# Splitting the first matmul of block 0 into three single-pass products, and re-timing the weight conversion's buffers, in a fused attention + FFN + FFN kernel

## The chip, the cores and the metric

One core of a Trainium2 chip (trn2) runs the whole program. The metric is device time in microseconds; the kernel before has a median of 902.7 us over three runs (900.95 to 904.78).

## What is computed

Pooled attention gives x (2304 tokens by 512), which goes through two feed-forward layers. Cut to what matters:

```python
k_p = k.reshape(B, H, Sp, 8, D).mean(axis=3); v_p = ...
attn = softmax(scale * q @ k_p^T);  x = attn @ v_p          # 2304 x 512
h = x @ moe_w_in;   g = where(h >= 1, h, where(h <= -1, 0, (h + 1)**2 / 4));  x = g @ moe_w_out
h = x @ moe2_w_in;  g = max(h, 0) + log1p(exp(-|h|));                         out = g @ moe2_w_out
```

Weights are 512 x 2048 and 2048 x 512. They arrive as 64-bit words, so each value has to be put together on ScalarE, VectorE (and GpSimd for the second layer) before TensorE can use it.

## The kernel before

The tokens are cut into five blocks (`BLK`: 4, 4, 4, 3, 3 tiles of 128 tokens). For each block, the first layer walks over 16 chunks of 128 hidden units. Chunk c of block j is iteration n = 16j + c of the main loop (L773). One iteration issues, on TensorE, the products of h (`emit_g1`, L496: four tiles of 128 along d_model) and then, two chunks late, the products of y (`emit_g2`, L537). Between them stand the activation (`act`, L516) and whatever `background` (L749) has due in that half step: two half steps `hs` make an iteration.

Block 0 is different (`whole`, L492). Its products use the fp32 weights and fp32 x as they are, one fp32 matmul per 128 x 128 weight tile, which the profile shows as two records each. From block 1 on each product is made of three matmuls of rounded parts (type fp32r): weight high by x high, weight high by x low, weight low by x high. The parts of a weight come from `split1` (L154): a copy with rounding on ScalarE (`whi`, L158), then a subtraction on VectorE (`wlo`, L160). In the kernel before, `split1` runs once per iteration: for the first two weight halves at the end of block 0, for the other 14 in block 1.

During block 0 the first layer's weights are also converted (`convert1`, L140): two ScalarE operations (L113, L116), then five on VectorE (L120, L121, L125, L148, L150) for each half weight. Each half weight is loaded by `w_load`; even and odd halves in `USE` (L133) belong to w_in and w_out in turn. Half `m` odd (m = 2i - 1) is needed by the products of h of chunks 2i and 2i + 1. The attention of block 1 (`tile_gen`, L400) and the pooling of the next batch's keys and values (`kv_gen`, L377; the reductions are L345) run between these operations.

From half step `CONV2` = 54 on, the second layer's weights are converted in 32 units (`convert2`, L174). `tick` (L667) advances the units under a budget of VectorE/ScalarE time (`credit`), starting a new one every `PITCH` = 3.1 half steps, if fewer than four of its buffers are in `held`. Each unit takes a buffer `a` (four of them); two units of w_in also make four sums in a tile `t` (L203 to L207). Every result is split into a high part in `b` (three buffers, L237) and a low part written over its source (L228), and both are stored to HBM (`wid`, `wod`) from the SP queue (L232 for the high part, L222 for the low part one tick later), because the second layer (L841 on) reads them from there (`wi_load`, `wo_load`). `held` drops a buffer as soon as its store has been issued. The tiles `t`, and all weights, take slots of one pool of 33 (`slot`).

All engines run in the order in which this program is written (`manual_schedule`), so an instruction that waits holds all that stands behind it on its engine. The pool's slots and the buffers make an instruction wait until the last reader of the earlier contents, stores included, is done.

Of the kernel before, what the change touches and what calls it, by code (L numbers as in the profile page):

```python
# [7 lines left out]
FP32 = mybir.dt.float32  # L8
FP32R = mybir.dt.float32r
# [3 lines left out]
ACTF = mybir.ActivationFunctionType  # L13
# [17 lines left out]
def pooled_attention_ffn_ffn(ctx, tc, q, k, v, v0, w1, w2, out):  # L31
# [24 lines left out]
    )  # L56

    CONV2, PITCH = 54, 3.1

    BUDGET = ((0.0, 0.0), (1.0, 2.5), (1.2, 2.5), (0.9, 1.9), (0.9, 1.9))  # L60
    T0 = [sum(BLK[:j]) for j in range(NB)]
# [41 lines left out]
    wi = {}  # L103
    wo = {}
    x2 = {}

    def slot(shape, dtype, name):
        return wpool.tile(shape, dtype, tag="w", name=name)
# [45 lines left out]
    def split1(m):  # L154

        hi, lo = (slot([128, 2, DM], FP32R, n) for n in ("whi", "wlo"))
        f = wt[USE[m]]
        nc.scalar.activation(out=hi, in_=f, func=ACTF.Copy)  # L158
        yield
        nc.vector.tensor_tensor(out=lo, in0=f, in1=hi.bitcast(FP32), op=ALU.subtract)  # L160
        wt[USE[m]] = (hi, lo)
        yield
# [6 lines left out]
            nc.sync.dma_start(out=raw[n], in_=src)  # L169

    left = {}
    held = []

    def convert2(n):  # L174
# [12 lines left out]
        st_load(n + 2)  # L187
        yield 0.7
        af = a.bitcast(FP32)
        nc.vector.tensor_tensor(out=af, in0=af, in1=l, op=ALU.add)  # L190
        yield 0.8 if r and not part else 0.0
        if part:
            jobs = [(n, af, lambda m: [(wod[:, h, m, r, :], slice(0, DM))])]
        elif r == 0:
            left[h] = af
            return
        else:

            b0, b1 = left.pop(h), af
            b11, b21, b12, b22 = (b[:, o:o + QK] for b in (b0, b1) for o in (0, QK))  # L200
            t = slot([128, 4, QK], FP32, "t")
            t3, t2, t4, t1 = (t[:, m, :] for m in range(4))
            nc.vector.tensor_tensor(out=t1, in0=b12, in1=b11, op=ALU.subtract)  # L203
            nc.vector.tensor_tensor(out=t3, in0=b22, in1=b12, op=ALU.subtract)
            yield 0.8
# [3 lines left out]
            tf = t.rearrange("p m f -> p (m f)")  # L209
            jobs = [  # L210
                (n - 1, b0, lambda m: [(wid[:, h, o, m, :], slice(x, x + QK)) for o, x in ((0, 0), (5, QK))]),
                (None, tf[:, 0:2 * QK], lambda m: [
                    (wid[:, h, 1 + o, m, :], slice(o * QK, (o + 1) * QK)) for o in range(2)]),
                (None, tf[:, 2 * QK:4 * QK], lambda m: [
                    (wid[:, h, 3 + o, m, :], slice(o * QK, (o + 1) * QK)) for o in range(2)]),
                (n, b22, lambda m: [(wid[:, h, 6, m, :], slice(0, QK))]),
            ]
        old = done = None
        stores = []
        for k, f, dst in jobs + [(None, None, None)] * 2:  # L220
            for d, x in stores:
                nc.sync.dma_start(out=d, in_=x)  # L222
            if done is not None:
                held.remove(done)
            stores, done = [], None
            if old:
                done, fo, hi, to = old
# [3 lines left out]
                for d, x in to(0):  # L231
                    nc.sync.dma_start(out=d, in_=hi.bitcast(FP32)[:, x])  # L232
                stores = [(d, fo[:, x]) for d, x in to(1)]
                old = None
            if f is not None:
                hi = es2.cv.tile([128, DM], FP32R, tag="b", bufs=3, name="b")[:, 0:f.shape[1]]
# [255 lines left out]
    def whole(j):  # L492

        return j == 0

    def emit_g1(j, c):  # L496
        n = 128 * BLK[j]
        h = ps["h"].tile([128, TB], FP32, tag="h", name="h")[:, 0:n]
        done = 0
        for kk in range(KD):  # L500
            cols = slice(kk * 128, (kk + 1) * 128)
            if whole(j):
                ops = ((wt[0, c // 2][:, c % 2, cols], xs[j][0].bitcast(FP32)),)
            else:
                wh, wl = (t[:, c % 2, cols] for t in wt[0, c // 2])
                xh, xl = xs[j]
                ops = ((wh, xh), (wh, xl), (wl, xh))
            for a, b in ops:
                nc.tensor.matmul(  # L509
                    out=h, lhsT=a, rhs=b[:, kk, 0:n],  # L510
                    start=(done == 0), stop=(done == len(ops) * KD - 1),
                )
                done += 1
        return h
# [150 lines left out]
    credit = [0.0]  # L665

    def tick(start):  # L667
        late = False
        for item in list(flight):
            late = late or item[1] > credit[0]  # L670
            if not (late and item[1]):
                credit[0] -= item[1]
                item[1] = next(item[0], None)
                item[2] += 1
                if item[1] is None:
                    flight.remove(item)
# [86 lines left out]

    pend = []
    acts = {}
    splits = []

    def step(key):
# [4 lines left out]
    for n in range(NB * NC):  # L773
# [20 lines left out]
            step(n - 2)  # L794
        if hot and c + 1 < NC:
            next(c1[c + 1])
        if hs == CONV2 - 4:
            st_load(0)
            st_load(1)
# [116 lines left out]
```

## Time and profile before

| | |
|---|---|
| median of 3 runs | 902.7 us (900.95 to 904.78) |
| the profiled execution | 907.54 us |
| its span (first to last instruction) | 905.7 us |
| TensorE busy | 878.4 us, 97% |
| TensorE weight load | 717.3 us, 79% |
| VectorE busy | 636.3 us, 70% |
| ScalarE busy | 508.4 us, 56% |
| GpSimd busy | 44.9 us, 5% |
| mean granted TensorE clock | 0.988 |

TensorE is busy for nearly all of the span, so the time can fall in two ways only: fewer microseconds of matmuls, or fewer of the gaps in which TensorE waits. A gap's row in the timeline names the instruction that ended it. A busy TensorE may also run at half its clock (the column PEclk).

### The profile page before, as it was taken

The page shows a single profiled execution, that of the slowest core. Times are in us where ns is not written, and L with a number is a line of the kernel's source. Part 1 is how long each engine was busy: PE and PEld are TensorE (multiplying, and loading weights), DVE is VectorE, ACT ScalarE, POOL GpSimd, SP SyncE. Part 2 cuts the span into 40 slices and gives each one's busy share as a digit, 9 for nine tenths or more (in the row PEclk, how much of TensorE's full clock was granted, in tenths as well). Part 3 has the DMA queues.
Part 4 walks back from the last instruction along what each step waited for, and adds up shares of the span by engine and source line. Part 5 has one row for each costly group of instructions (what it writes and reads, how often), then busy time and mean ns, then how long its engine had stood idle before and what let it go on. Part 6 is the DMA issues. An engine that isn't in the chain of part 4 may idle for free. (4 is left out here: it accounts for less than half of the span.)

```text
span 905.7 us, 12186 instructions
## 1 busy us (share of the span) xinstructions
PE 878.4 (97%) x4490; PEld 717.3 (79%) x4490; DVE 636.3 (70%) x951; ACT 508.4 (56%) x925; POOL 44.9 (5%) x41
## 2 busy tenths in 40 slices
PE   8899999999998999999999999999999999999996
PEld 4444445688886788889999988889899898889885
DVE  6798774665667768677888678585778766665763
ACT  3856653555654546656577565554657464554551
POOL 0000000000111112111121100000000000000000
PEclk8999999999999999999999999999999999999999
DMA  7745330110164545743585796548197456496202
GB/s 255 286 156 190 124 141 10 60 59 12 59 187 136 177 140 166 227 160 99 199 307 193 253 338 234 175 137 312 51 346 258 128 163 233 151 357 203 92 1 70
DMA packets 66411, 154.94 MB, mean 171 GB/s; under 512 B 6896, under 2 KB 27376, under 8 KB 64304
## 3 DMA queue, kind: packets, MB, share of 16 engines
q1 hardware_dynamic: 66352, 154.17, 50.4%
q8 instruction: 35, 0.57, 0.3%
q14 instruction: 24, 0.20, 0.1%
HBM read 121.63 MB, written 32.51 MB: 170 GB/s over the span
## 5 line engine op out<-in xcount | busy, mean ns | idle before, releaser
L590 PE MATMUL h<-xfh,wi 128*128 128x384 f32 x544 | 160.3, 337 | 1.9 <-DVE h L858 1.2
L627 PE MATMUL y<-whi,gl 128*128 128x512 f32 x288 | 114.1, 396 | 0.0
L627 PE MATMUL y<-wlo,gh 128*128 128x512 f32 x288 | 113.7, 395 | 0.0
L627 PE MATMUL y<-whi,gh 128*128 128x512 f32 x288 | 112.0, 389 | 0.0
L590 PEld LDWEIGHTS h<-xfh,wi 128*128 128x128 f32 x544 | 100.8, 188 | 9.4 <-DVE h L858 2.6
L551 PE MATMUL y<-gl,whi 128*128 128x512 f32 (+1 forms) x256 | 95.1, 371 | 9.7 <-DVE gl L535 9.6
L551 PE MATMUL y<-gh,whi 128*128 128x512 f32 (+1 forms) x256 | 96.0, 375 | 0.5 <-ACT gh L533 0.5
L509 PE MATMUL h<-xh,whi 128*128 128x512 f32 (+1 forms) x256 | 95.4, 372 | 0.0
L551 PE MATMUL y<-gh,wlo 128*128 128x512 f32 (+1 forms) x256 | 93.9, 367 | 0.0
L509 PE MATMUL h<-xh,wlo 128*128 128x512 f32 (+1 forms) x256 | 92.8, 362 | 0.0
L509 PE MATMUL h<-xl,whi 128*128 128x512 f32 (+1 forms) x256 | 92.7, 362 | 0.0
L590 PE MATMUL h<-xfl,wi 128*128 128x384 f32 x272 | 91.9, 338 | 0.0
L601 ACT ACTIVATE e<-h 128x768 f32<-128x768 f32 x48 | 40.1, 840 | 84.2 <-DVE h L858 84.2
L858 DVE TENSOR_TENSOR h<-h,s 128x384 f32<-128x384 f32 x72 | 40.0, 556 | 65.8 <-PE h L590 65.6
L519 ACT ACTIVATE t<-h 128x512 f32<-128x512 f32 (+1 forms) x80 | 44.0, 550 | 61.5 <-PE h L509 60.0
L185 POOL TENSOR_TENSOR l<-l,st 128x512 bf16<-128x512 bf16 x32 | 43.5, 1360 | 465.0 <-DVE st L125 410.7
L627 PEld LDWEIGHTS y<-whi,gl 128*128 128x128 f32 x288 | 54.0, 187 | 11.6
L551 PEld LDWEIGHTS y<-gl,whi 128*128 128x128 f32 x256 | 48.8, 191 | 17.3 <-DVE gl L535 12.7
L509 PE MATMUL h<-xh,wf 128*128 128x512 f32 x128 | 59.4, 611 | 0.7 <-ACT xh L479 0.7
L627 PEld LDWEIGHTS y<-whi,gh 128*128 128x128 f32 x288 | 54.1, 188 | 6.3
L627 PEld LDWEIGHTS y<-wlo,gh 128*128 128x128 f32 x288 | 54.0, 187 | 6.3
L551 PE MATMUL y<-g,wf 128*128 128x512 f32 x128 | 58.1, 596 | 0.4 <-DVE wf L150 0.4
(96 smaller groups left out, 1666.2 us busy)
## 6 DMA issues: line engine op xcount, KB each, us to landing
wi<-wid SPq DMA_DIRECT2D x72, 512.0 KB, 5.4
raw<-in_w SPq DMA_DIRECT2D x16, 1024.0 KB, 4.8
st<-in_w SPq DMA_DIRECT2D x32, 512.0 KB, 4.2
whi<-wod SPq DMA_DIRECT2D x24, 512.0 KB, 4.5
wlo<-wod SPq DMA_DIRECT2D x24, 512.0 KB, 5.1
wid<-b SPq DMA_DIRECT2D x56, 128.0 KB, 2.9
wi<-wid SPq DMA_DIRECT2D x24, 256.0 KB, 5.2
kv<-in_k SPq DMA_DIRECT2D x16, 288.0 KB, 5.0
```

The costliest lines, as they stand in the source:

```text
L185: nc.gpsimd.tensor_tensor(out=l, in0=l, in1=e, op=ALU.mult)
L509: nc.tensor.matmul(out=h, lhsT=a, rhs=b[:, kk, 0:n], start=(done == 0), stop=(done == len(ops) * KD - 1),)
L519: nc.scalar.activation(out=g, in_=h, func=ACTF.Relu, bias=1.0)
L551: nc.tensor.matmul(out=y[:, 0:128 * BLK[j]], lhsT=a, rhs=b, start=(c == 0 and n == 0), stop=(c == NC - 1 and n == len(ops) - 1),)
L590: nc.tensor.matmul(out=o, lhsT=a[:, cols], rhs=b[:, kk, :], start=(p in FRESH and done == 0), stop=(done == 5), skip_group_check=True,)
L601: nc.scalar.activation(out=e, in_=h, func=ACTF.Abs)
L627: nc.tensor.matmul(out=y, lhsT=a, rhs=b, start=(m == w == n == 0), stop=(last and n == 2))
L858: nc.vector.tensor_tensor(out=h, in0=o, in1=keep[x], op=ALU.add)
```

## The change

1. The products of h of block 0, from chunk 4 on (12 of 16 chunks), use three fp32r matmuls per weight tile instead of one fp32 matmul. `emit_g1` takes that path wherever the weight has been split. x of block 0 is split by the new `split_x0` in two halves (iterations 2 and 3), the high part into the unused second tile of x, the low part into two slots.
2. Six calls of `split1` (halves 3, 5, 7, 9, 11, 13) move from block 1 into block 0 at chunks 3, 5, ... 13. Halves 0, 1 and 2 are split in the last three iterations of block 0, the remaining seven in chunks 2 to 8 of block 1. Each of these ten takes 1.2 us off the conversion's `credit`.
3. The second layer's conversion starts ten half steps earlier (`CONV2` 54 to 44, five chunks).
4. `convert2` makes its parts in another order: the four sums `t` first, then the two sources. A store of two 256-wide pieces is one DMA (256 KB) instead of two (128 KB each). `held` drops a buffer two ticks after its last store is issued, and a new `t` is not begun until three ticks after the last one's store (`landing`, `sums`).

```diff
-    CONV2, PITCH = 54, 3.1
+    CONV2, PITCH = 44, 3.1
...
-        yield 0.8 if r and not part else 0.0
+        yield SUMS if r and not part else 0.0
...
+            assert not sums
+            sums.append(h)
             t = slot([128, 4, QK], FP32, "t")
...
             jobs = [
-                (n - 1, b0, lambda m: [(wid[:, h, o, m, :], slice(x, x + QK)) for o, x in ((0, 0), (5, QK))]),
-                (None, tf[:, 0:2 * QK], lambda m: [
-                    (wid[:, h, 1 + o, m, :], slice(o * QK, (o + 1) * QK)) for o in range(2)]),
-                (None, tf[:, 2 * QK:4 * QK], lambda m: [
-                    (wid[:, h, 3 + o, m, :], slice(o * QK, (o + 1) * QK)) for o in range(2)]),
-                (n, b22, lambda m: [(wid[:, h, 6, m, :], slice(0, QK))]),
+                (None, t[:, 0:2, :], wid[:, h, 1:3, :, :].rearrange("p o m f -> p m o f")),
+                ("t", t[:, 2:4, :], wid[:, h, 3:5, :, :].rearrange("p o m f -> p m o f")),
+                (n - 1, b0.rearrange("p (o f) -> p o f", o=2),
+                 wid[:, h, 0:6:5, :, :].rearrange("p o m f -> p m o f")),
+                (n, b22, wid[:, h, 6, :, :]),
             ]
...
-            if done is not None:
-                held.remove(done)
+                if k0 is not None:
+                    landing.append([3 if k0 == "t" else 2, k0])
...
+    def split_x0(n):
+
+        x = xs[0][0].bitcast(FP32)[:, 2 * n:2 * n + 2, :]
+        xh = xs[0][1][:, 2 * n:2 * n + 2, :]
+        nc.scalar.activation(out=xh, in_=x, func=ACTF.Copy)
+        yield
+        xl0[n] = slot([128, 2, TB], FP32R, "xl")
+        nc.vector.tensor_tensor(out=xl0[n], in0=x, in1=xh.bitcast(FP32), op=ALU.subtract)
...
-            if whole(j):
-                ops = ((wt[0, c // 2][:, c % 2, cols], xs[j][0].bitcast(FP32)),)
+            if type(w) is not tuple:
+                ops = ((w[:, c % 2, cols], xs[j][0].bitcast(FP32)[:, kk, 0:n]),)
             else:
-                wh, wl = (t[:, c % 2, cols] for t in wt[0, c // 2])
-                xh, xl = xs[j]
+                wh, wl = (t[:, c % 2, cols] for t in w)
+                xh, xl = (x[:, kk, 0:n] for x in xs[j]) if j else (xs[0][1][:, kk], xl0[kk // 2][:, kk % 2])
                 ops = ((wh, xh), (wh, xl), (wl, xh))
...
     def tick(start):
+        for x in list(landing):
+            x[0] -= 1
+            if not x[0]:
+                landing.remove(x)
+                sums.clear() if x[1] == "t" else held.remove(x[1])
         late = False
         for item in list(flight):
-            late = late or item[1] > credit[0]
+            late = late or item[1] > credit[0] or item[1] == SUMS and bool(sums)
...
+    SPLITS = {(0, NC - 3): 0, (0, NC - 2): 1, (0, NC - 1): 2}
+    SPLITS.update({(1, 2 + i): m for i, m in enumerate((4, 6, 8, 10, 12, 14, 15))})
...
+        if hot and c in (2, 3):
+            xg = split_x0(c - 2)
+            next(xg)
+
+        if hot and 3 <= c < NC - 2 and c % 2:
+            w0 = split1(c)
+            next(w0)
...
+        if hot and c in (2, 3):
+            next(xg, None)
+        if hot and 3 <= c < NC - 2 and c % 2:
+            next(w0)
         background(hs + 1)

-        if j == 0 and c >= NC - 2 or j == 1 and c < NC - 2:
-            splits = [split1((c + 2) % NC)]
+        if (j, c) in SPLITS:
+            splits = [split1(SPLITS[j, c])]
             next(splits[0])
+            credit[0] -= 1.2
```

The order of the instructions shows what moves. On TensorE around the products of h of chunk 4 (the third to the sixth row before; the row before them ends the products of y of chunk 1), before:

```order
L551 MATMUL y_445<-g,wf 128x512
L408 MATMUL a<-kp,q 64x72 x16
L509 MATMUL h<-xh,wf 128x512 x4
L551 MATMUL y_442<-g,wf 128x512
L551 MATMUL y_443<-g,wf 128x512
```

and now (here `xl` as moving operand stands both for the tile that holds x's high part and for the slot with its low part):

```order
L564 MATMUL y_446<-g,wf 128x512
L412 MATMUL a<-kp,q 64x72 x16
L523 MATMUL h<-xl,whi 128x512 x2
L523 MATMUL h<-xl,wlo 128x512
L523 MATMUL h<-xl,whi 128x512 x2
L523 MATMUL h<-xl,wlo 128x512
L523 MATMUL h<-xl,whi 128x512 x2
L523 MATMUL h<-xl,wlo 128x512
L523 MATMUL h<-xl,whi 128x512 x2
L523 MATMUL h<-xl,wlo 128x512
L564 MATMUL y_443<-g,wf 128x512
```

Four fp32 matmuls became twelve; the third of them already needs the weight's low part `wlo`.

On VectorE, in iterations 2 and 3 of block 0 (conversion of half weights 3 and 4, key and value pooling), before:

```order
L150 TENSOR_TENSOR wf<-wf,l 128x1024
L345 TENSOR_REDUCE ks<-kv 128x72
L525 SCALAR_TENSOR_TENSOR g<-t,h 128x512
L120 TENSOR_SCALAR b<-wf 128x1024
L121 SCALAR_TENSOR_TENSOR wf<-wf,b 128x1024
L125 TENSOR_SCALAR b<-wf 128x1024
L345 TENSOR_REDUCE ks<-kv 128x72
L148 TENSOR_TENSOR l<-l,b 128x1024
L150 TENSOR_TENSOR wf<-wf,l 128x1024
L345 TENSOR_REDUCE ks<-kv 128x72
L525 SCALAR_TENSOR_TENSOR g<-t,h 128x512
```

and now:

```order
L151 TENSOR_TENSOR wf<-wf,l 128x1024
L507 TENSOR_TENSOR xl<-xh,xl 128x1024
L349 TENSOR_REDUCE ks<-kv 128x72
L538 SCALAR_TENSOR_TENSOR g<-t,h 128x512
L121 TENSOR_SCALAR b<-wf 128x1024
L122 SCALAR_TENSOR_TENSOR wf<-wf,b 128x1024
L126 TENSOR_SCALAR b<-wf 128x1024
L349 TENSOR_REDUCE ks<-kv 128x72
L149 TENSOR_TENSOR l<-l,b 128x1024
L151 TENSOR_TENSOR wf<-wf,l 128x1024
L507 TENSOR_TENSOR xl<-xh,xl 128x1024
L161 TENSOR_TENSOR wlo<-wf,whi 128x1024
```

Three operations over 1024 elements are new in the queue (two `xl`, one `wlo`), and the `wlo` that chunk 4 waits for stands behind all of them.

In the SP queue, where the first unit pair of the second layer's weights is stored, before (near the end of block 1, with the loads of keys `kv` and of weights `st` between):

```order
L232 DMA wid<-b 128x256 x2
L339 DMA kv<-in_k 128x576
L222 DMA wid<-a 128x256 x2
L232 DMA wid<-b 128x256 x2
L169 DMA st<-in_w 128x1024
L222 DMA wid<-t 128x256 x2
L232 DMA wid<-b 128x256 x2
L572 DMA y1d<-y 128x4x128 x4
L339 DMA kv<-in_k 128x576
L222 DMA wid<-t 128x256 x2
L232 DMA wid<-b 128x256
```

and now:

```order
L235 DMA wid<-b 128x2x256
L170 DMA st<-in_w 128x1024
L226 DMA wid<-t 128x2x256
L235 DMA wid<-b 128x2x256
L226 DMA wid<-t 128x2x256
L235 DMA wid<-b 128x2x256
L226 DMA wid<-a 128x2x256
L235 DMA wid<-b 128x256
L226 DMA wid<-a 128x256
```

Pairs of stores became single ones, the sums `t` go before the sources `a`, and the block's `y1d` stores no longer stand in the middle of them. In the whole program the stores of converted weights are 96 instead of 144.

## Rows read from the trace of the kernel before

**Rows 1.** Busy time by stretch: us, TensorE, its weight load, VectorE, ScalarE, GpSimd, granted clock, DMA.

```profile
43.50:58.20 14.70, 14.69 (x64) 6.69 (x65) 14.46 (x20) 8.20 (x11) 0.00 (x0) 1.00 0.61 221
58.20:150.00 91.80, 91.27 (x348) 44.16 (x347) 68.32 (x90) 51.87 (x117) 0.00 (x0) 1.00 0.36 126
```

**Rows 2.** Timeline of TensorE in block 0: start, us, line, operands, records, [idle before, releaser].

```profile
107.28 3.60 PE L551 MATMUL y<-g,wf 128*128 128x512 f32 x8
...
114.15 3.60 PE L551 MATMUL y<-g,wf 128*128 128x512 f32 x8
```

**Rows 3.** Timeline of TensorE, last chunks of block 0's y beside block 1's h.

```profile
153.23 3.59 PE L551 MATMUL y<-g,wf 128*128 128x512 f32 x8
...
159.40 3.59 PE L551 MATMUL y<-g,wf 128*128 128x512 f32 x8
```

**Rows 4.** Timeline of TensorE at chunks 4 and 6 of block 0.

```profile
54.67 3.70 PE L509 MATMUL h<-xh,wf 128*128 128x512 f32 x8
...
69.64 1.04 PE L452 MATMUL a<-ident,e 128*72 128x128 f32 x8 [0.53 <-DVE e L448]
...
74.05 1.15 PE L466 MATMUL a<-pT,vp 72*64 72x64 f32 x32
```

**Rows 5.** Timeline of VectorE in iterations 3 to 6 of block 0.

```profile
48.60 1.22 DVE L150 TENSOR_TENSOR wf<-wf,l 128x1024 f32<-128x1024 f32 x1
49.74 0.74 DVE L345 TENSOR_REDUCE ks<-kv 128x72 f32<-128x576 f32 x1
...
56.11 0.74 DVE L345 TENSOR_REDUCE ks<-kv 128x72 f32<-128x576 f32 x1
...
65.11 0.69 DVE L525 SCALAR_TENSOR_TENSOR g<-t,h 128x512 f32<-128x512 f32 x1 [1.22 <-ACT t L520]
...
68.74 0.76 DVE L448 TENSOR_TENSOR e<-e,sm 128x576 f32<-128x576 f32 x1
...
71.28 0.68 DVE L525 SCALAR_TENSOR_TENSOR g<-t,h 128x512 f32<-128x512 f32 x1
```

**Rows 6.** Timeline of ScalarE, the first exponential of block 1's first tile.

```profile
61.40 0.32 ACT L441 ACTIVATE e<-a,mn 128x72 f32<-128x72 f32 x1 [4.03 <-DVE mn L427]
```

**Rows 7.** Groups of instructions: the low part of a weight (count, busy us, mean ns, idle).

```profile
L160 DVE TENSOR_TENSOR wlo<-wf,whi 128x1024 fp32r<-128x1024 f32 x16 | 20.3, 1269 | 4.0 <-ACT whi L158 4.0
```

**Rows 8.** Timeline of VectorE at the start of block 1.

```profile
165.43 1.23 DVE L160 TENSOR_TENSOR wlo<-wf,whi 128x1024 fp32r<-128x1024 f32 x1 [0.26 <-ACT whi L158]
```

**Rows 9.** Timeline of TensorE: gaps in blocks 1 to 4.

```profile
167.31 0.50 PE L551 MATMUL y<-gl,whi 128*128 128x512 f32 x1 [1.36 <-DVE gl L535]
...
279.69 0.50 PE L551 MATMUL y<-gl,whi 128*128 128x512 f32 x1 [4.14 <-DVE gl L535]
...
306.66 0.50 PE L551 MATMUL y<-gh,whi 128*128 128x512 f32 x1 [0.46 <-ACT gh L533]
...
405.87 1.22 PE L466 MATMUL a<-pT,vp 72*64 72x128 f32 x16 [1.57 <-ACT pT L458]
...
511.90 0.44 PE L551 MATMUL y<-gl,whi 128*128 128x384 f32 x1 [0.70 <-DVE gl L535]
```

**Rows 10.** Timeline of VectorE: the longest wait for a store.

```profile
275.95 0.43 DVE L203 TENSOR_TENSOR t<-a 128x256 f32<-128x256 f32 x1 [5.94 <-DMA wid<-t]
```

**Rows 11.** Timeline of ScalarE: two waits for a store.

```profile
304.88 0.67 ACT L113 ACTIVATE a<-st 128x512 f32<-128x512 f32 x1 [4.21 <-DMA wid<-a]
...
403.70 0.66 ACT L113 ACTIVATE a<-st 128x512 f32<-128x512 f32 x1 [2.86 <-DMA wid<-a]
```

**Rows 12.** Busy time by stretch behind the gaps that end at 279.69 and 405.87.

```profile
279.00:282.00 3.00, 2.31 (x7) 1.83 (x8) 2.93 (x7) 2.97 (x6) 0.00 (x0) 0.73 0.04 8
282.00:285.00 3.00, 3.00 (x11) 2.39 (x10) 2.90 (x6) 0.77 (x2) 1.16 (x1) 0.70 0.36 103
406.00:408.00 2.00, 2.00 (x19) 1.70 (x19) 0.02 (x1) 1.97 (x6) 0.00 (x0) 0.67 0.58 198
408.00:410.00 2.00, 2.00 (x8) 2.00 (x7) 2.00 (x5) 1.60 (x3) 0.00 (x0) 0.50 0.09 26
```

More of the change, by code (lines that the diff above doesn't have):

```diff
@@ L105, in pooled_attention_ffn_ffn @@
     x2 = {}
+    xl0 = {}
     def slot(shape, dtype, name):
@@ L171, in pooled_attention_ffn_ffn @@
     left = {}
+    SUMS = 0.81
     held = []
+    sums = []
+    landing = []
     def convert2(n):
@@ L190, in convert2 @@
         nc.vector.tensor_tensor(out=af, in0=af, in1=l, op=ALU.add)
-        yield 0.8 if r and not part else 0.0
+        yield SUMS if r and not part else 0.0
         if part:
-            jobs = [(n, af, lambda m: [(wod[:, h, m, r, :], slice(0, DM))])]
+            jobs = [(n, af, wod[:, h, :, r, :])]
         elif r == 0:
@@ L208, in convert2 @@
             yield 0.0
-            tf = t.rearrange("p m f -> p (m f)")
             jobs = [
-                (n - 1, b0, lambda m: [(wid[:, h, o, m, :], slice(x, x + QK)) for o, x in ((0, 0), (5, QK))]),
-                (None, tf[:, 0:2 * QK], lambda m: [
-                    (wid[:, h, 1 + o, m, :], slice(o * QK, (o + 1) * QK)) for o in range(2)]),
-                (None, tf[:, 2 * QK:4 * QK], lambda m: [
-                    (wid[:, h, 3 + o, m, :], slice(o * QK, (o + 1) * QK)) for o in range(2)]),
-                (n, b22, lambda m: [(wid[:, h, 6, m, :], slice(0, QK))]),
-            ]
-        old = done = None
-        stores = []
+                (None, t[:, 0:2, :], wid[:, h, 1:3, :, :].rearrange("p o m f -> p m o f")),
[3 more added lines that the diff above has]
+                (n, b22, wid[:, h, 6, :, :]),
+            ]
+        old = store = None
         for k, f, dst in jobs + [(None, None, None)] * 2:
-            for d, x in stores:
+            if store:
+                k0, d, x = store
                 nc.sync.dma_start(out=d, in_=x)
-            if done is not None:
-                held.remove(done)
-            stores, done = [], None
+                if k0 is not None:
+                    landing.append([3 if k0 == "t" else 2, k0])
+            store = None
             if old:
-                done, fo, hi, to = old
+                k0, fo, hi, to = old
                 nc.vector.tensor_tensor(
@@ L230, in convert2 @@
                 )
-                for d, x in to(0):
-                    nc.sync.dma_start(out=d, in_=hi.bitcast(FP32)[:, x])
-                stores = [(d, fo[:, x]) for d, x in to(1)]
+                nc.sync.dma_start(out=to[:, 0], in_=hi.bitcast(FP32))
+                store = (k0, to[:, 1], fo)
                 old = None
             if f is not None:
-                hi = es2.cv.tile([128, DM], FP32R, tag="b", bufs=3, name="b")[:, 0:f.shape[1]]
+                hi = es2.cv.tile([128, DM], FP32R, tag="b", bufs=3, name="b")
+                hi = hi.rearrange("p (o f) -> p o f", o=2) if len(f.shape) == 3 else hi[:, 0:f.shape[1]]
                 nc.scalar.activation(out=hi, in_=f, func=ACTF.Copy)
@@ L499, in emit_g1 @@
         done = 0
+        w = wt[0, c // 2]
         for kk in range(KD):
             cols = slice(kk * 128, (kk + 1) * 128)
-            if whole(j):
-                ops = ((wt[0, c // 2][:, c % 2, cols], xs[j][0].bitcast(FP32)),)
-            else:
-                wh, wl = (t[:, c % 2, cols] for t in wt[0, c // 2])
-                xh, xl = xs[j]
+            if type(w) is not tuple:
+                ops = ((w[:, c % 2, cols], xs[j][0].bitcast(FP32)[:, kk, 0:n]),)
+            else:
+                wh, wl = (t[:, c % 2, cols] for t in w)
+                xh, xl = (x[:, kk, 0:n] for x in xs[j]) if j else (xs[0][1][:, kk], xl0[kk // 2][:, kk % 2])
                 ops = ((wh, xh), (wh, xl), (wl, xh))
@@ L509, in emit_g1 @@
                 nc.tensor.matmul(
-                    out=h, lhsT=a, rhs=b[:, kk, 0:n],
-                    start=(done == 0), stop=(done == len(ops) * KD - 1),
+                    out=h, lhsT=a, rhs=b, start=(done == 0), stop=(done == len(ops) * KD - 1),
                 )
```

## The prediction

> **What bounds the kernel now.** I read the table of engines first: TensorE is busy 97% of the span, so time can only come out of its matmuls or out of its gaps. Then the busy time by stretch of block 0 [rows 1]: from 43.5 to 150 us TensorE has no gap worth the name, but in the first 14.7 us VectorE is busy too, 14.46 of 14.70; after 58.2 it has room (68.32 of 91.80). So block 0 is bound by TensorE, with a VectorE just behind it at the start. Third, the timeline of TensorE for the gaps of blocks 1 to 4 [rows 9], and what the engine that ended each gap had waited for [rows 8, 10, 11]. The reader is to see that a wait for a store on VectorE or ScalarE, both run in program order, comes out a little later as a gap of TensorE, and that TensorE may run at half its clock behind it [rows 12].
>
> **Twelve chunks in three passes.** One chunk of fp32 products of h plus one of y takes 114.15 - 107.28 = 6.87 us [rows 2]. The border of the blocks shows what the change makes of it: fp32 products of y beside split products of h take 159.40 - 153.23 = 6.17 us [rows 3]. That is 0.70 us less per chunk; twelve chunks give **-8.4 us**. Half of 6.87 is 3.43 for an fp32 chunk, so a split one takes 6.17 - 3.43 = 2.74 us, 0.228 us a matmul.
>
> **What VectorE takes back at the start.** The change puts two splits of x and one `wlo` into VectorE's queue before chunk 4, and then one `wlo` per two chunks. The nearest row is `wlo` itself, 1.27 us [rows 7]; from one start to the next such an operation takes 49.74 - 48.60 = 1.14 us [rows 5]. The queue there is back to back, so nothing hides them. The first split of x shifts all behind it by 1.14 us; the weight conversion whose last operation ended at 56.11 [rows 5] ends at 57.25, the second split of x at 58.39, `wlo` at about 59.7. TensorE is at chunk 4 at 54.67 [rows 4] and can issue two matmuls before it needs `wlo`: it waits from 55.1 to 59.7, **+4.5 us**, and finishes the chunk at 59.7 + 10 x 0.228 = 61.9.
>
> The same backlog, 3 x 1.14 = 3.4 us, meets chunk 6. Attention's exponentials wait for a maximum in VectorE's queue [rows 6], the activation stands behind them on ScalarE, and VectorE waits for it: the row at 65.11 [rows 5]: the whole chain moves by 3.4 us. The scaling at 68.74 ends at 72.9. TensorE gets there at 61.9 + (69.64 - 0.53 - 54.67) - 3.43 - 0.70 = 72.2 [rows 4], so its wait of 0.53 us grows by about 0.1. The `wlo` of chunk 6 now stands where VectorE was at 71.28, that is at 74.7, and ends at 75.9. TensorE has issued two matmuls by 74.3: **+1.7 us**. Chunk 6 then ends at 78.2 instead of 74.05 [rows 4], 4.1 us late. From there VectorE has room: the stretch up to 150 holds 68.32 us of work plus five `wlo`, 5.7, in 91.8 less about 7 [rows 1]. The remaining nine chunks give 9 x 0.70 = 6.3, and block 1 starts **2.1 us earlier**. Bounds for block 0: -8.4 if nothing waits, and -8.4 + 8 x 1.27 = +1.8 if every added operation is paid.
>
> The ScalarE halves (two of x, six `whi`) run ahead of VectorE there, which is the later one; if it were not, they would cost a microsecond each. The gap of 4.5 us should also cost clock. Behind the gap of 4.14 us the clock was granted at 0.73 and 0.70 [rows 12]: 2.31 x 0.27 + 3.00 x 0.30 = 1.5 us lost. Here these 1.5 us fall before chunk 6, where TensorE would wait 1.7 us anyway: nothing is added.
>
> **Start of block 1.** The gap of 1.36 us [rows 9] is ended by the low part of g, which stands on VectorE right behind the `wlo` at 165.43 [rows 8]. That split is gone from iterations 17 and 18, 1.14 us on VectorE and its wait of 0.26: **-1.3 us** (between -1.4 and 0).
>
> **The conversion's buffers.** The longest gap, 4.14 us [rows 9], goes back to VectorE, which waited 5.94 us [rows 10] to write a new `t` over a slot whose store had not landed. With `sums` a `t` is begun three ticks after the last one's store, and its stores come first: I take it all, 4.14 + 1.5 of clock = **-5.6 us**. The gaps of 0.46 and 1.57 us follow ScalarE's waits of 4.21 and 2.86 us for a store out of `a` [rows 11]; behind the second the clock fell to 0.67 and 0.50 [rows 12], 2 x 0.33 + 2 x 0.50 = 1.7 us. Two ticks after the store (a half step is about 3 us) `a` should be free, but transfers were slow just there: I take half of 0.46 + 1.57 + 1.7, **-1.9 us**.
>
> **End of the conversion.** It starts five chunks earlier, and in the order of the program the last unit's first operation stands in chunk 72, not 76. That takes VectorE's load off the end of block 4: the gap of 0.70 us [rows 9], **-0.7 us**. What is late next: the earlier units now stand beside seven splits, attention of block 2 and the loads of keys, and `landing` makes new units start later; loads and stores fall at other times. No row shows this. I put it between 0 (no new gap; work in another place shortens no matmul, so no gain) and the sum of gaps and clock that the buffers cost before, 5.6 + 3.7 = 9.3 us. VectorE has room before 276 us, so I am nearer the lower end: **+1.5 us**. Merged stores (96 in place of 144) shorten SP's queue, which nothing waits for by itself: 0.
>
> **Sum.** -2.1 - 1.3 - 5.6 - 1.9 - 0.7 + 1.5 = -10.1 us, on the profiled execution's 907.5 us: 897.4. That execution was 4.8 us above the median of the runs; I carry the difference over to the median: 902.7 - 10.1 = **892.6 us**. Its own range, with the second term anywhere between its parts, is 887 to 898.
>
> **Rivals.**
> - *The waits move* (2 in 10). The stores land when SP and the DMA engines let them, and a start five chunks earlier only meets other traffic. For it: the gaps of rows 9 have different owners. Against it: the longest has one owner, which the change names. Then only block 0 and the start of block 1 remain: 902.7 - 2.1 - 1.3 = 899.3.
> - *VectorE's queue holds nobody* (1 in 10): -8.4 instead of -2.1, 886.3. Against it stands the order of the queue; for it only that ScalarE's or a load's waits may have made VectorE late before, and don't now.
> - *VectorE becomes the bound of block 0* (8 in 100). In the first 14.7 us it is busy 98% [rows 1]. If all eight added operations are paid, block 0 changes by +1.8 and the sum by 3.9: 896.5. The Trainium skill ("Perfetto Trace Analysis", Identifying the Most-Contended Engine) takes the engine with the highest occupancy as the one that decides, which speaks against adding VectorE work here; by it the sum for that first stretch would be this rival's. The trace agrees with it for 14.7 us and not for the rest of block 0 (74%).
> - *Slower: the stores come late after all* (6 in 100). One mechanism: a wait on VectorE or ScalarE longer than TensorE's cover, one chunk of products (12 x 0.228 = 2.7 us), becomes a gap with half clock behind it, 5.6 us each time as at 275.95 [rows 10, 12]. The eight pairs of w_in units can each do this; with the earlier gaps staying and two more of them: 902.7 - 3.4 + 11.2 = 910.5. It decides from the second extra one on.
>
> **How the numbers follow.** A measurement here tells from no change what is beyond about 0.5%, 4.5 us: 898.2 and 907.2 are the borders. The forecast has 56 in 100, nearly all of it below 898.2; with the second and most of the third rival and a quarter of the first this makes faster 0.74, within 0.5% 0.20, slower 0.06. The range, 885 to 900, holds the forecast, the first three rivals and the bounds of block 0, and leaves out the slow one.
>
> **What would show it.** Right: split chunks 0.70 us shorter; a gap of about 4.5 us at chunk 4 ended by `wlo`, one of 1 to 2 us at chunk 6, none after; block 1's first products at about 148; no gap of over 2 us from there to the second layer; no VectorE wait on a `t` store. Wrong: more than two gaps in block 0, or block 0 shorter by over 5 us (VectorE did not hold chunk 4), or gaps of over 2 us with PEclk below 1 in blocks 1 to 4 that follow a wait for a store.

## The result, and the profile after

The changed kernel takes **894.68 us** (median of 4 runs, 894.32 to 894.78), the kernel before in the same comparison 903.47 us (4 runs, 900.95 to 904.78). The ratio is 0.9905, with a 95% interval of 0.9882 to 0.9929: 8.6 us less, between 6.4 and 10.7. By the bound of 0.5% that the prediction used it is faster. 892.6 us and a range of 885 to 900 had been predicted.

The table of engines of the changed kernel:

```profile
span 893.0 us, 12212 instructions
...
PE 866.1 (97%) x4538; PEld 722.9 (81%) x4538; DVE 638.4 (71%) x953; ACT 511.0 (57%) x927; POOL 44.4 (5%) x41
```

TensorE is busy 12.3 us less than before, its share is the same. The two profiled executions differ by 12.7 us of span, more than the medians do. The windows from 10 to 20 us, ahead of every instruction that the change touches, tell why; the kernel before first, then the changed one (columns as in rows 1):

```profile
10.00:20.00 10.00, 10.00 (x54) 5.37 (x52) 9.54 (x21) 4.56 (x19) 0.00 (x0) 0.66 0.87 302
```

```profile
10.00:20.00 10.00, 9.45 (x74) 5.45 (x73) 9.54 (x22) 6.59 (x22) 0.00 (x0) 1.00 0.80 299
```

The profiled execution of before had a spell at a lower clock there: 10 x 0.34 = 3.4 us, no part of the change. So traces are compared below stage by stage, and times by the ratios.

**Block 0.** Timeline of TensorE, changed kernel; the rows answer to [rows 2, 4]:

```profile
50.21 0.73 PE L523 MATMUL h<-xl,whi 128*128 128x512 f32 x2
55.19 0.80 PE L523 MATMUL h<-xl,wlo 128*128 128x512 f32 x1 [4.25 <-DVE wlo L161]
...
71.50 0.50 PE L523 MATMUL h<-xl,wlo 128*128 128x512 f32 x1 [0.16 <-DVE wlo L161]
...
82.61 3.59 PE L564 MATMUL y<-g,wf 128*128 128x512 f32 x8
...
88.78 1.45 PE L564 MATMUL y<-g,wf 128*128 128x512 f32 x3
...
143.92 0.80 PE L523 MATMUL h<-xh,whi 128*128 128x512 f32 x1
```

A pair of chunks takes 88.78 - 82.61 = 6.17 us where it took 6.87. Chunk 4 stops after two matmuls for 4.25 us, until `wlo` is there. VectorE's timeline shows the queue behind that wait, with no idle time in it:

```profile
51.64 1.22 DVE L151 TENSOR_TENSOR wf<-wf,l 128x1024 f32<-128x1024 f32 x1
52.79 1.22 DVE L507 TENSOR_TENSOR xl<-xh,xl 128x1024 fp32r<-128x1024 f32 x1
53.92 1.22 DVE L161 TENSOR_TENSOR wlo<-wf,whi 128x1024 fp32r<-128x1024 f32 x1
```

The clock falls within the gap, is at half (0.50) behind it and is back at 1.00 by 60 us:

```profile
51.00:55.00 4.00, 0.00 (x0) 0.00 (x0) 3.96 (x5) 1.13 (x1) 0.00 (x0) 0.77 0.25 66
55.00:58.00 3.00, 2.81 (x7) 2.23 (x8) 2.96 (x5) 0.00 (x0) 0.00 (x0) 0.50 0.96 325
60.00:63.00 3.00, 3.00 (x9) 1.33 (x7) 2.80 (x4) 2.65 (x17) 0.00 (x0) 1.00 0.00 0
```

From the start of chunk 4 to block 1's first product it is 143.92 - 50.21 = 93.71 us; before it was 150.09 - 54.67 = 95.42. Block 0 gained 1.7 us.

**Blocks 1 to 4.** The gaps of [rows 9] in blocks 1 and 2 are gone, and the one at the end of block 4. The two longest that are left are of the kind of 405.87 there, behind ScalarE's copy of `pT`, and the clock stayed at 1.00 behind both:

```profile
390.60 0.66 PE L470 MATMUL a<-pT,vp 72*64 72x128 f32 x8 [1.42 <-ACT pT L462]
...
411.96 0.33 PE L470 MATMUL a<-pT,vp 72*64 72x128 f32 x2 [1.27 <-ACT pT L462]
```

ScalarE's waits for loads and stores between 180 and 510 us (us in total, times, longest), before and after:

```profile
ACT a L113 <- DMA wid<-a: 10.6, 3, 4.2
ACT a L113 <- DMA st<-in_w: 9.9, 7, 3.2
ACT b L237 <- DMA wid<-b: 7.3, 3, 4.3
ACT a L113 <- DMA wod<-a: 6.0, 2, 5.2
```

```profile
ACT a L114 <- DMA st<-in_w: 21.3, 9, 4.0
ACT b L241 <- DMA wid<-b: 15.7, 8, 2.4
ACT a L114 <- DMA wod<-a: 1.8, 1, 1.8
```

The waits for `a` are gone or short, as is VectorE's 5.94 us for `t` [rows 10]. In their place stand waits for the loads `st` and for the stores out of `b`: 33.8 us before, 38.8 after, but in shorter pieces. The stretch of blocks 3 and 4, before and after (the same work, from block 3's first h to the second layer's first product), shows that TensorE is not better off there. It stands idle 153.95 - 148.37 = 5.6 us before and 154.38 - 147.94 = 6.4 us after:

```profile
359.99:513.94 153.95, 148.37 (x889) 142.53 (x888) 120.36 (x218) 98.67 (x214) 25.68 (x19) 0.99 0.61 204
```

```profile
344.96:499.34 154.38, 147.94 (x890) 140.94 (x888) 114.21 (x208) 94.63 (x204) 22.51 (x17) 1.00 0.58 199
```

Stages of the traces in us (block 0: first h to block 1's first y; blocks 1 and 2: to block 3's first h; blocks 3 and 4: to the second layer's first product; second layer: to the start of the last matmul). The block 0 of before holds another 1.7 us at half clock, in the first 24 records of h.

| kernel | block 0 | blocks 1, 2 | blocks 3, 4 | second layer |
|---|---|---|---|---|
| before | 134.7 | 194.4 | 154.0 | 383.9 |
| after | 131.9 | 185.6 | 154.4 | 385.7 |
| e1_block0 | 131.8 | 191.4 | 153.7 | 384.5 |
| e2_buffers | 133.5 | 186.8 | 151.9 | 385.7 |
| e3_both_54 | 132.0 | 185.3 | 154.9 | 385.4 |
| e4_block0_44 | 132.2 | 187.2 | 148.1 | 383.9 |
| f1_no_sums | 132.3 | 185.6 | 152.0 | 385.3 |
| f2_no_held | 131.9 | 188.7 | 166.7 | 384.9 |
| f3_spaced | 131.9 | 185.3 | 150.6 | 384.7 |
| f4_merged | 131.9 | 185.7 | 164.6 | 384.5 |
| g1_swap | 131.8 | 189.3 | 148.1 | 384.1 |
| g2_late_pool | 135.6 | 187.7 | 147.9 | 384.1 |
| g3_start38 | 132.1 | 189.4 | 154.9 | 383.8 |
| h1_gpsimd | 133.7 | 186.2 | 148.1 | 384.5 |

### The profile page after: what moved, and what is told of

The parts are those of the page before. It is cut to its first block, busy times and chain, and to the rows that moved or that the text cites. A ratio compares the mean times of both kernels' runs of the same rounds, so it can differ in the third digit from the quotient of the medians.

```text
span 893.0 us, 12212 instructions
## 1 busy us (share of the span) xinstructions
PE 866.1 (97%) x4538; PEld 722.9 (81%) x4538; DVE 638.4 (71%) x953; ACT 511.0 (57%) x927; POOL 44.4 (5%) x41
## 4 chain that ended last, share of the span: by engine, by line
PE 73%; DVE 11%; DMA 7%; ACT 7%; issue 2%; SPq 0%; POOL 0%; ACTq 0%; DVEq 0%
PE y L640 21%; PE h L603 18%; PE y L564 15%; PE h L523 14%; DMA st<-in_w 2%; DMA wid<-b 2%; PE a L412 2%; PE a L470 2%; DMA x<-y1d 1%; PE a L456 1%; DVE gl L548 1%; DVE ks L349 1%; DVE wf L122 1%; ACT e L445 1%; DVE t L538 1%
## 5 line engine op out<-in xcount | busy, mean ns | idle before, releaser
L523 PE MATMUL h<-xl,whi 128*128 128x512 f32 (+1 forms) x352 | 126.2, 381 | 0.0
L523 PEld LDWEIGHTS h<-xl,whi 128*128 128x128 f32 x352 | 66.4, 190 | 10.8 <-issue 2.4
```

The source lines that it names most:

```text
L523: nc.tensor.matmul(out=h, lhsT=a, rhs=b, start=(done == 0), stop=(done == len(ops) * KD - 1),)
```

## The experiments

Each ratio is to runs of the kernel before on the same chip (medians 901.3 to 901.7 us, so 0.001 is 0.9 us).

### Which part brings the time: e1 to e4

**Block 0 alone.** The kernel before with items 1 and 2 of the change:

```diff
+    SPLITS = {(0, NC - 3): 0, (0, NC - 2): 1, (0, NC - 1): 2}
...
+        if hot and 3 <= c < NC - 2 and c % 2:
+            w0 = split1(c)
+            next(w0)
```

> Block 0's part alone: the split products, split_x0 and the moved splits with their 1.2 us of credit; the conversion of the second layer starts at half step 54 with its old stores and buffers. My theory (parts add up): -2.1 us in block 0 and -1.3 us at the start of block 1, so -3.4 us (ratio 0.996), the gap of about 4.25 us at chunk 4 ended by wlo, and the gap of about 4 us behind a wait for a store of t still there. Rival 1 (the stores are all the gain, VectorE eats up what block 0 saves): 0 us. Rival 2 (block 0 is the whole gain): -8 us, with no gap over 2 us in block 1's conversion.

Measured: 898.99 us, ratio 0.9969 (0.9955 to 0.9982), -2.8 us. The gap at chunk 4 is 4.25 us, and the wait for `t` is still there, with its gap of TensorE:

```profile
267.23 0.43 DVE L204 TENSOR_TENSOR t<-a 128x256 f32<-128x256 f32 x1 [4.60 <-DMA wid<-t]
```

```profile
270.95 0.50 PE L561 MATMUL y<-gl,whi 128*128 128x512 f32 x1 [2.79 <-DVE gl L545]
```

Both rivals fall: block 0 is neither nothing nor all.

**The buffers alone.** The kernel before with item 4:

```diff
-            if done is not None:
-                held.remove(done)
+                if k0 is not None:
+                    landing.append([3 if k0 == "t" else 2, k0])
```

> The buffers alone: order of the parts, merged stores, landing and sums; block 0 in fp32 and the conversion from half step 54 on as before. My theory: the gap behind the wait for a store of t goes, with its clock, and half of those behind a: -5.6 - 1.9 = -7.5 us (ratio 0.992), no wait of VectorE for a store of t. Rival 1 (the early start and the moved splits, not the buffers, end that wait): between -1 and +1 us, the wait still there. Rival 2 (single stores of 256 KB land later than pairs): slower, +1 to +5 us.

Measured: 896.96 us, ratio 0.9950 (0.9933 to 0.9966), -4.5 us. The wait for `t` is gone, so the buffers do end it. But 7.5 us is outside the interval. Waits for `st` grew from 9.9 to 23.1 us, and others appeared in blocks 3 and 4, as this one on ScalarE:

```profile
456.88 0.63 ACT L240 ACTIVATE b<-a 128x512 fp32r<-128x512 f32 x1 [5.72 <-DMA wid<-b]
```

**The change without the earlier start.** The changed kernel with

```diff
-    CONV2, PITCH = 44, 3.1
+    CONV2, PITCH = 54, 3.1
```

> The change without the earlier start: everything of it, but the conversion from half step 54 on. My theory (parts add up): -3.4 - 7.5 = -10.9 us, that is 2 us faster than the whole change's -8.8, since the early start was put at +1.5 - 0.7 = +0.8. Rival (the early start gives the buffers the time that they need): -3 to -5 us, with gaps of over 2 us behind waits for stores.

Measured: 893.76 us, ratio 0.9916 (0.9896 to 0.9936), -7.6 us. The parts add up (2.8 + 4.5 = 7.3), each smaller than thought. With the buffers in place the earlier start does nothing that can be measured: the interval of the whole change overlaps this one.

**Block 0 and the earlier start, old buffers.** The kernel before with items 1, 2 and 3:

```diff
-    CONV2, PITCH = 54, 3.1
+    CONV2, PITCH = 44, 3.1
```

> Block 0's part and the earlier start (half step 44), with the old buffers and stores. My theory (the buffers end the wait for t): -3.4 + 0.8 = -2.6 us, with a wait of VectorE of several us for a store of t and a gap of TensorE behind it. Rival (the early start moves the conversion to where stores land in time): about -8 us, with no gap over 2 us and no VectorE wait for t over 3 us.

Measured: 888.52 us, ratio 0.9854 (0.9838 to 0.9870), -13.2 us: the rival was right, and went further than it said. Start 44 alone is worth 0.0115, 10.4 us, and the new buffers on top of it cost 4.6 us. The wait for `t` shrinks to 1.40 us, and no gap of TensorE stands behind it. The next gap, 0.90 us, comes 22 us later, when VectorE had no wait for a store:

```profile
234.85 0.43 DVE L204 TENSOR_TENSOR t<-a 128x256 f32<-128x256 f32 x1 [1.40 <-DMA wid<-t]
```

```profile
257.08 0.50 PE L561 MATMUL y<-gl,whi 128*128 128x512 f32 x1 [0.90 <-DVE gl L545]
```

ScalarE's waits in this kernel, beside the 21.3 and 15.7 us of the changed one:

```profile
ACT b L238 <- DMA wid<-b: 8.2, 4, 4.1
ACT a L114 <- DMA wod<-a: 2.9, 3, 1.1
ACT a L114 <- DMA wid<-b: 1.0, 1, 1.0
ACT a L114 <- DMA st<-in_w: 0.5, 2, 0.3
```

Against the changed kernel the stages show -6.3 us in blocks 3 and 4, -1.8 in the second layer and +1.6 in blocks 1 and 2.

The wait for `t` is not all that the start is worth: against e1 the stages show -4.2 us in blocks 1 and 2, where that wait stood, and -5.6 in blocks 3 and 4. In e1 ScalarE waits 16.8 us in all for `wid<-a` and 11.1 us for `st`; here the first is gone and the second is 0.5. Why stores and loads land in time when the conversion starts earlier, no run shows.

### What the new buffers cost: f1 to f4

The distances between the first operations of successive units, from ScalarE's timeline (us, the first 16):

```
after         10.2 11.5 8.2 23.2 1.1 23.2 1.7 7.3 10.6 13.4 11.1 4.9 8.5 17.2 4.9 4.6
e4_block0_44  10.2 11.5 8.2 14.6 5.2 15.5 4.6 9.1  5.0 19.9  8.2 7.2 9.0 14.1 5.7 5.9
```

After a pause the units follow each other closely, because `due` lets a late start be caught up. Two buffers hold `st`, and a load takes 3.8 us to land (the median between 365 and 392 us). The SP queue of the changed kernel issued three loads of `st` one after another from 380.85 to 392.21, and ScalarE waited for them:

```profile
385.20 0.67 ACT L114 ACTIVATE a<-st 128x512 f32<-128x512 f32 x1 [3.38 <-DMA st<-in_w]
```

**Without `sums`.**

```diff
-            late = late or item[1] > credit[0] or item[1] == SUMS and bool(sums)
+            late = late or item[1] > credit[0]
```

> The changed kernel without the wait of a new t for three ticks (sums); held buffers still wait two ticks, stores merged, parts in the new order, start at 44. My theory now: the rules make units of the conversion stand still for 13 to 23 us and then follow each other by 1 to 5 us, faster than a load of st lands (3.8 us), and ScalarE waits for st (21.3 us in all, against 0.5 with the old rules). If sums does it, starts spread out, waits for st fall under 5 us, blocks 3 and 4 last about 148 us instead of 154.4, and the time is about -13 us against before (ratio 0.986). If held does it (rival), nothing changes here: -8 to -9 us (0.991). Rival 2 (without sums the wait for a t's store returns): a VectorE wait for t over 4 us, -5 us or slower.

Measured: 894.00 us, ratio 0.9926 (0.9900 to 0.9952), -6.7 us. The interval overlaps the changed kernel's and does not meet e4's, as the first rival had it: `sums` alone is not what costs the 4.6 us, and it is not needed either, for no wait for `t` came back. Waits for `st` halved to 11.0 us all the same.

**Without the delay of `held`.**

```diff
-                if k0 is not None:
-                    landing.append([3 if k0 == "t" else 2, k0])
+                if k0 == "t":
+                    landing.append([3, k0])
+                elif k0 is not None:
+                    held.remove(k0)
```

> The changed kernel with a buffer dropped from held as soon as its store is issued, as before; sums still waits three ticks. If held makes the bunches: starts spread out, waits for st under 5 us, blocks 3 and 4 about 148 us, -13 us against before (0.986). If sums does (my first guess): -8 to -9 us (0.991), waits for st near 21 us. Rival 2 (held was needed): ScalarE waits of 3 to 6 us for a store out of a and -5 us or slower.

Measured: 910.56 us, ratio 1.0087 (1.0059 to 1.0115), 7.8 us slower than before. Of my theory one sign came, waits for `st` under 5 us (4.9), but the time went the other way and its second rival holds: `held` is needed. ScalarE waits for stores out of `a`, then TensorE for ScalarE, and behind that the clock is 0.54; ScalarE, TensorE and a window of this kernel:

```profile
469.80 0.66 ACT L114 ACTIVATE a<-st 128x512 f32<-128x512 f32 x1 [6.55 <-DMA wod<-a]
```

```profile
471.99 0.69 PE L566 MATMUL y<-gh,whi 128*128 128x384 f32 x1 [5.39 <-ACT gh L548]
474.29 0.69 PE L566 MATMUL y<-gl,whi 128*128 128x384 f32 x1 [1.61 <-DVE gl L550]
```

```profile
474.00:478.00 4.00, 3.71 (x12) 3.71 (x13) 3.38 (x7) 3.09 (x6) 1.25 (x1) 0.54 0.00 0
```

That store was one of many under way: in the stretch from 455 to 472 us, with the second layer's loads of `x` in it, issue to landing takes about twice the 3.5 us that `wod<-a` took between 365 and 392 us in the changed kernel:

```profile
x<-y1d SPq DMA_DIRECT2D x3, 384.0 KB, 7.6
...
wod<-a SPq DMA_DIRECT2D x1, 256.0 KB, 8.3
```

**Units spaced out.** The changed kernel, with a start at the earliest two half steps after the last:

```diff
-            due[0] += (len(units) < todo) * PITCH
+            due[0] = max(due[0] + PITCH, hs + 2) if len(units) < todo else due[0]
```

> The changed kernel with one more rule: a unit of the conversion starts at the earliest two half steps (about 5.5 us) after the one ahead, so a pause is not caught up in a bunch. My theory (bunches that outrun the loads cost the time, whatever makes the pauses): waits for st fall to under 8 us, blocks 3 and 4 about 150 us, -11 to -13 us against before (0.986 to 0.988). Rival (pauses cost, not bunches): no gain, -8 us, or slower than the changed kernel, since the conversion then ends later and meets the second layer: -4 us.

Measured: 890.47 us, ratio 0.9872 (0.9853 to 0.9891), -11.5 us, as the theory said. Waits for `st` are 1.6 us in all, blocks 3 and 4 take 150.6 us, and TensorE stands idle for 2.6 us of them, against 6.4 in the changed kernel:

```profile
348.40:498.98 150.58, 147.97 (x889) 142.71 (x888) 112.91 (x205) 96.52 (x207) 22.65 (x17) 0.99 0.55 190
```

Pauses are still there (23.2 us, and three of over 14 in the first 16), so it is the bunches that cost, not the pauses. The interval touches that of the changed kernel at its edge (0.9891 and 0.9882); the wait rows are the stronger evidence.

**Neither wait.** Both edits, f1's and f2's, in one kernel; merged stores, the new order and the early start remain.

> The changed kernel with neither wait: only merged stores, the new order of the parts and the early start are left of the conversion's changes. My theory (the two waits make the pauses): as the kernel with old buffers and early start, -13 us (0.986), units spread, waits for st under 3 us. Rival (single stores of 256 KB and the new order, with ScalarE's waits for b, 15.7 us in all, are what costs): -8 to -9 us (0.991), waits for b over 12 us in all.

Measured: 906.10 us, ratio 1.0046 (1.0031 to 1.0060), 4.1 us slower than before: neither expectation. Units still pause (17.9, 19.3 and 24.3 us) and bunch at first, and ScalarE waits 11.5 us for `wod<-a`, with a gap of 4.39 us behind the longest. The half step in which each of the 32 units starts follows from the program's own counting (`tick`, `credit`, `held`), without the chip, and the order of ScalarE's operations in the traces fits it:

```
e4_block0_44  44 48 51 54 57 60 63 66 69 72 76 79 82 85 89 91 94 97 100 103 106 110 113 116 119 122 125 128 131 134 137 141
f4_merged     44 48 51 54 59 60 65 66 69 72 78 79 82 85 89 91 94 97 100 103 106 110 114 116 119 122 125 128 131 134 137 141
after         44 48 51 54 61 62 69 70 72 75 80 84 85 88 93 96 97 99 106 108 109 111 119 121 122 124 130 133 134 136 142 145
```

So the first pauses come without the two rules, from the new order of the parts (`tick` counts parts, so merging two stores into one does not enter). The rules make the later ones: from the thirteenth unit on f4 starts its units where e4 does, all but one, while in the changed kernel the pairs go on to the end. There, between 345 and 500 us, ScalarE's waits for `st` are 14.3 us in the changed kernel, 4.1 in f1, and none of over 0.3 us in f4.

What f4 loses to e4 in blocks 3 and 4 (164.6 us against 148.1) can then not come from pauses. ScalarE waits there 4.91 and 5.98 us for a store out of `a`, and the mean clock of the stretch is 0.96 against 1.00. Against e4 the new order and the merged stores alone cost 0.0192, 17.3 us, and `held` and `sums` together win 12.7 of them back. Which of the two makes ScalarE wait, order or merging, was not tried apart and stays open.

### What limits block 0: g1, g2, h1, and an earlier start: g3

All four start from e4 (888.52 us).

**One swap in VectorE's queue.**

```diff
-        if hot and c in (2, 3):
-            next(xg, None)
         if hot and 3 <= c < NC - 2 and c % 2:
             next(w0)
+        if hot and c in (2, 3):
+            next(xg, None)
```

> Base: the kernel with block 0's part, the early start and the old buffers (-13.0 us against before). One swap on VectorE: the wlo that chunk 4 waits for is issued ahead of the second split of x, not behind it. My theory (TensorE waits there for VectorE's queue, which is back to back): the gap at chunk 4 falls by one such operation, 1.14 us, from 4.6 to about 3.5 us; chunk 6 then waits as much longer for its wlo unless the activation in between gets earlier, so the start of block 1 gains 0 to 1.1 us: -13 to -14 us (ratio 0.9845 to 0.9855). Rival (the weight's high part on ScalarE or the load is what is late): the gap stays at 4.3 to 4.6 us.

Measured: 889.18 us, ratio 0.9845 (0.9820 to 0.9870): as e4. Timeline of TensorE:

```profile
53.76 0.50 PE L520 MATMUL h<-xl,wlo 128*128 128x512 f32 x1 [3.12 <-DVE wlo L161]
...
68.44 0.41 PE L453 MATMUL a<-ident,e 128*72 128x128 f32 x2 [1.74 <-ACT vp L357]
...
71.20 0.50 PE L520 MATMUL h<-xl,wlo 128*128 128x512 f32 x1 [1.22 <-DVE wlo L161]
```

The gap at chunk 4 fell to 3.12 us, by about the 1.14 us of one operation (from 4.25 in the changed kernel, 4.61 in e4). So TensorE does wait for the order of VectorE's queue. What was won is waited for again before and in chunk 6 (2.96 us against 0.78), and block 1 begins 0.4 us earlier.

**Pooling later.**

```diff
-    PLAN = ((7, 6), (5, 6), (4, 8), (2, 8))
+    PLAN = ((10, 5), (5, 6), (4, 8), (2, 8))
...
-        (2, 3, 4, 5, 6, 7, 8, 9, 10, 11),
+        (7, 8, 8, 9, 10, 11, 11, 12, 12, 13),
```

and the swap of g1.

> The same base with the swap, and the pooling of block 1's keys and values five half steps later, so that five reductions of 0.67 us leave VectorE's queue ahead of chunk 4's wlo, and three of them with the first attention tile's work (3.8 us in all) go behind chunk 6's wlo. My theory: wlo ends 3.3 + 1.1 = 4.4 us earlier, the gap at chunk 4 falls to under 0.5 us and its clock loss goes; chunk 6 waits 1 to 2 us; block 1 starts about 4 us earlier, -16 to -18 us against before (0.980 to 0.982). Rival (VectorE has no room in all of block 0, the wait only moves): gaps of 3 us or more in chunks 6 to 10, -13 us (0.986). Rival 2 (attention of block 1, now five half steps apart, ends late): a gap at the start of block 1, -11 us or slower.

Measured: 894.86 us, ratio 0.9916 (0.9884 to 0.9948). The gaps at chunks 4 and 6 are down to 1.59 and 0.27 us, the way the theory has it, the first not as far. But the attention tiles, now five half steps apart, wait for each other and for the keys:

```profile
61.72 0.29 PE L409 MATMUL a<-kp,q 64*64 64x72 f32 x4 [1.55 <-ACT kp L353]
...
85.93 0.33 PE L409 MATMUL a<-kp,q 64*128 64x72 f32 x2 [1.42 <-DVE xl L483]
```

The second kind comes three times, and block 0 is 3.4 us longer than in e4. The mechanism of rival 2 (attention in the way), not its place.

**Start 38.**

```diff
-    CONV2, PITCH = 44, 3.1
+    CONV2, PITCH = 38, 3.1
```

> The same base, conversion from half step 38 on instead of 44. The start at 44 instead of 54 was worth 10.4 us with the old buffers (-2.8 to -13.0 us). If that came from units that leave blocks 3 and 4, where an iteration is shorter and the last loads and stores crowd (15 units there against 18, 148.1 us against 153.7), three chunks more take two more out: about -1 to -3 us more, -14 to -16 us (0.982 to 0.984). Rival (44 is already early enough, what is left of waits is elsewhere): -12.5 to -13.5 us. Rival 2 (it now meets the seven splits at the start of block 1 on VectorE): gaps of over 1 us before 200 us, -10 us or slower.

Measured: 895.45 us, ratio 0.9927 (0.9901 to 0.9952): 6.6 us slower than e4. Earlier is not better by itself: pauses of 23.7 and 23.8 us follow, waits for `st` are 14.2 us in all, the longest 6.67 at 292.58 us, and blocks 3 and 4 are back at 154.9 us with only 14 units in them (15 in e4). So e4's gain is not the number of units that leave blocks 3 and 4. Nor is it shown to be how evenly they start: by the program this kernel starts its last units about three half steps apart, as e4 does, and so does the kernel before. The cause stays open. Rival 2 had the time, not the place.

**GpSimd takes the splits of x.**

```diff
-        nc.vector.tensor_tensor(out=xl0[n], in0=x, in1=xh.bitcast(FP32), op=ALU.subtract)
+        nc.gpsimd.tensor_tensor(out=xl0[n], in0=x, in1=xh.bitcast(FP32), op=ALU.subtract)
```

> Base: the kernel with block 0's part, the early start and the old buffers (-13.0 us against before). Both splits of x into their low parts go from VectorE to GpSimd, which has nothing to do in block 0 (1.37 us for 512 elements of bf16 later on). My theory (what block 0 waits for is VectorE's work in total up to chunk 6, so that a swap inside the queue moved the wait and gained nothing, while work that leaves the queue counts): 2 x 1.14 = 2.3 us fewer, the gap at chunk 4 falls from 4.6 to about 2.3 us, that at chunk 6 does not grow, block 1 starts 2 us earlier, about -15 us against before (ratio 0.983). Rival (GpSimd is late, or slows VectorE down while it runs): the gap at chunk 4 is 4 us or more, ended by xl, or VectorE's operations beside it take longer: -11 to -13 us (0.9855 or more).

Measured: 893.05 us, ratio 0.9911 (0.9887 to 0.9936), -8.0 us: the rival's mechanism, and slower than its range. GpSimd's split, VectorE beside it, and TensorE at chunk 4:

```profile
41.70 2.87 POOL L504 TENSOR_TENSOR xl<-xh,xl 128x1024 fp32r<-128x1024 f32 x1 [39.59 <-ACT xl L501]
```

```profile
41.12 1.23 DVE L122 SCALAR_TENSOR_TENSOR wf<-wf,b 128x1024 uint32<-128x1024 uint32 x1
42.38 2.74 DVE L126 TENSOR_SCALAR b<-wf 128x1024 uint16<-128x1024 uint16 x1
```

```profile
57.25 0.79 PE L520 MATMUL h<-xl,wlo 128*128 128x512 f32 x1 [4.77 <-DVE wlo L161]
```

The operation of L126 takes 0.69 us otherwise; here it ended only after GpSimd had (44.57), 2.05 us late, and the same happened beside the second split. VectorE lost 4.1 us to save 2.3. The gap is ended by `wlo`, not `xl`. Block 0 is 1.5 us longer than in e4; the profiled execution took 890.0 us, the others, up to 895.7, left no trace, and the rest of the difference between the medians stays open.

## Why the prediction was right, and where it was wrong

- **Twelve chunks, -8.4:** right. The pair takes 6.17 us.
- **VectorE's backlog, a gap of 4.5 us at chunk 4 ended by `wlo`:** right: 4.25. `wlo` was to be ready 59.7 - 54.67 = 5.0 us after the chunk began; it was 55.14 - 50.21 = 4.9. g1 shows that the queue's order makes it. Chunk 6 was to wait 1.7 us and waited 0.16 in this execution (0.76 to 0.95 in e1, e4, f3 and f4, under 0.2 in e3, f1, f2 and g3). The clock cost more than 1.5 us (half of the 5 us from 55 to 60 is 2.5), and as forecast this was absorbed: chunk 6 then had less to wait. Block 0: -1.7 for -2.1. VectorE held TensorE in this stretch alone; over block 0 the gain came through.
- **Start of block 1, -1.3:** right, the gap of 1.36 us is gone, in e1 too; what that alone was worth was not measured. With block 0 this was -3.4; e1 measured -2.8 (-4.1 to -1.6).
- **The conversion's buffers, -7.5:** mechanism right, size wrong. Alone they gave -4.5 (-6.0 to -3.1). The wait for `t` and its gap went as told; what the step left out is that the rules make units bunch in blocks 3 and 4 and wait for `st` (f3, f4).
- **Merged stores, 0:** this step failed. It took only SP's queue into account, and the new order of the parts was given no cost either. Without the two rules, order and merging together cost 17.3 us (f4 against e4), and the rules win back only 12.7 of them.
- **The earlier start, -0.7 and +1.5 for new waits:** this step failed. Without the new buffers the start was worth -10.4 us, not +0.8; it all but ends the wait for `t` by itself, and more than half of its gain lies elsewhere, in blocks 3 and 4, for a reason that stays open. With them it is worth nothing measurable (e3 against the whole). I had added the two as separate terms. For the wait for `t` they are two cures of one ill, and the second costs: -2.8 - 10.4 + 4.6 = -8.6. That the prediction's -3.4 - 7.5 + 0.8 = -10.1 came near is luck: a cure put too large stood beside one put too small, and a cost was left out.
- **The sum's own range** was not 887 to 898: with the second term anywhere from -8.4 to +1.8 it comes to 886.3 to 896.5. The rows of gaps [rows 9] also leave out one of block 3, of 1.49 us at 374.93; the changed kernel has none like it there.
- **The rivals.** "The waits move" holds for blocks 3 and 4: TensorE stands idle there for 6.4 us, 5.6 before. "Slower: the stores come late" did not happen, but its mechanism is real: f2 shows it with one gap of 5.39 + 1.61 us and half clock behind, at 7.8 us slower. With the new order it is the delay of `held` that keeps it away.

The fastest version found is e4: block 0's products and the early start, with the conversion's buffers left alone, 888.52 us, ratio 0.9854 (0.9838 to 0.9870). By the ratios it is 4.6 us below the changed kernel, and the two intervals do not meet. g1 (0.9845) and f3 (0.9872) cannot be told from it.

## What to carry to other kernels

Before two edits that remove the same wait are summed, ask what each would do without the other, and time them apart: here either one ended or all but ended the wait, and both together were slower than the earlier start alone. Where each unit of a background task starts can be worked out from the program before it runs; pauses and bunches show there. Here a task that caught up after a pause ran faster than its loads; a smallest distance between starts costs one line. Moving an operation within a full queue moved the wait with it (g1). That work which leaves the queue would count was not shown: g2 and h1 lost elsewhere what they won there, h1 because VectorE was held up beside GpSimd.

## What the runs showed of the hardware

- GpSimd's subtraction over 1024 fp32 elements (2.87 and 3.15 us) stretched a VectorE operation with one 16-bit input from 0.69 to 2.74 and 2.75 us; it ended 0.55 us after GpSimd both times. The Trainium skill ("GPSIMD Engine Reference", Key points) says that GpSimd shares its SBUF interfaces with VectorE and names VectorE instructions in a 2-port mode or with two SBUF inputs. The trace agrees that the two engines contend, by the 2.05 us that L126 lost each time; in which mode L126 runs no row shows. The two-input operation of L122, already running when GpSimd began, kept its 1.23 us.
- The mean granted clock from 10 to 20 us was 0.66 in one execution and 1.00 in another, of the same instructions: 3.4 us that a comparison of two single traces would put down to the change. f3's profiled execution had the spell too (0.66).
- Gaps of 1.42 and 1.27 us in the changed kernel left the clock at 1.00, and so did the one of 1.49 us at 374.93 in the kernel before (1.00 from 375 to 378 us), while the gap of 1.57 us in the kernel before had 0.67 and 0.50 behind it [rows 12]. What makes the difference was not tried.
